# Gated mix of attention and an MLP: halves of value batches shared out over the turns of five, and the row-maximum product issued last in its slot

## The chip, the cores and the metric

The kernel runs on one core of one Trainium2 chip. The metric is the device time of one execution in microseconds (us), lower is better; the time given for the kernel is the median of its runs.

## The reference

```python
x = A_x                                             # 1 x 2048 x 448
g = sigmoid((x * gate_w).sum(-1, keepdims=True))
qkv = (x @ wqkv), split into q, k, v of 16 heads, 28 wide
p = softmax(q @ k.T * 28 ** -0.5)                   # per head, 2048 x 2048
a = (p @ v, heads side by side) @ wo
h = gelu(layernorm(x) @ w1 + b1)                    # 2048 x 1792, tanh form
b = h @ w2 + b2
out = g * a + (1 - g) * b
```

All inputs and outputs are 32-bit floats.

## The kernel before

The program has three stages. The first makes queries, keys and values; the second is the MLP; the third is the attention with the output projection. Each of the products of the first two stages is split into strips of 32 rows and mixed with row-maximum products by a planner (`Strips`). The change is in the third stage alone, from the function `early` on; what stands ahead of it in the program is the same.

**Units.** In the third stage the work of TensorE is written out by hand. The 16 heads form 4 groups of 4, the 2048 queries 4 chunks of 512. A *column* is one group with one chunk, and there are 16. A column holds 64 *units*: a unit is one head `j` of the group with one tile `k` of 128 keys, against the chunk's 512 queries, so 1024 units in all. Units are numbered `u`, with `j = u % 4`. Head `j` lies in the rows 32j to 32j+31 of the operands, so products of different heads use different row strips of TensorE.

**Scores.** A unit's scores are three products into one bank of PSUM: high part of the keys by high part of the queries (in traces `yh,ka` or `yh,kb`), low part of the keys by high of the queries (`yh,la`, `yh,lb`), and high of the keys by low of the queries (`yl,ka`, `yl,kb`). The first of the three has one row more than the head's 28, in which minus one meets the row's maximum, so that what lands in the bank is the score less its maximum. ScalarE then writes the exponentials of two or three banks at once to a tile `p` (L1164).

**Row maxima.** The maximum of each row of scores over all keys must be known before the column's scores are used. It comes from a product of its own, without splitting (L212, `kd,qd`), into one bank, which VectorE reduces (L214). Such a product with its reduction is called a *row maximum* here. `lone` (L1118) issues one, if its operands are loaded.

**Turns.** `turn_of` (L1131) takes the next 5 units, or 6 where fewer row maxima are still owed, or 7 where none are. The first half of the turn holds three units (four of seven), the second the others. Each half makes three passes over its units, one for each of the three products, then one exponential of the half's banks. Half and pass give six *slots*, 0 to 5. `extra` (L1146) names the slots of a turn that hold a row maximum, the head (from `u`) and the bank: in a turn of five slots 0, 3 and 5, in bank 6, the sixth of the score banks, and bank 6 again; in a turn of six slots 0 and 5, both in bank 6; in a turn of seven none. Scores use banks 0 to 5, values bank 7.

**Values.** A *batch* (L1169) is the four units of one tile of keys: four products of 32 columns of values (the stationary operand) by the units' exponentials, each into its own 32 partitions of bank 7, summed over the 16 tiles of keys of the column. A batch can be issued in two halves of 256 queries each. In the trace every value product appears as two records, so a batch is 8 records with 512 elements, a half batch 8 records with 256. After the last batch of a column `valued` copies the bank out on VectorE (L1026), sends the row of sums through DRAM (L1027, L1035, L1037 on SyncE's queue), and multiplies by its reciprocal on GpSimd (L1043).

**The order around the change.** The loop at L1181 takes a turn, runs what is due in that turn (`agenda`: loads, splits of keys and queries, closings of columns), then issues batches. `before` is the number of units that stood scored before this turn; a batch is open when its four units are among them. `quota` counts half batches. In turns of six and seven it is 3, or 4 when more than two batches are open; in turns of five it stays at 99, so every open batch is issued. After the last batch of a column the turn issues no more. The exponentials' tiles come from a pool with three buffers for each half (L955), so the tile of a turn takes the place of that of three turns before.

Each engine runs its own instructions in order, and waits for another by a semaphore; a waiting instruction holds up those behind it on its engine.

Of the kernel before, what the change touches and what calls it, by code (L numbers as in the profile page):

```python
# [35 lines left out]
def kernel(ctx: ExitStack, tc: tile.TileContext, xt, wqk, wv, wo, xk, w1, b1, w2, b2,  # L36
# [367 lines left out]
    class Strips:  # L404
# [28 lines left out]
        def at(self, t, fn, **uses):  # L433
            self.tasks.append((t, self.count, fn, uses))
            self.count += 1
# [473 lines left out]
    for b, m in enumerate((0, 3, 4)):  # L909
        x = QK(0, m)  # L910
# [32 lines left out]
    def turn_bank(i):  # L943
        return (i + shift) % 6

    def idle(n, b):
        for _ in range(n):
            nc.tensor.matmul(bk[:, b], khi[0][:, 0:P], khi[0][:, 0:CH], start=True, stop=True)  # L948
# [50 lines left out]
    def products(po, tt, groups):  # L999
        c, i = divmod(tt, TPC)  # L1000
        sl = slice(i * P, (i + 1) * P)
        for g in groups:
            h, l = (t[:, g, sl] for t in ohs[c])
            nc.tensor.matmul(po, h, woh[:, g], start=(g == 0), stop=False, skip_group_check=True)  # L1004
            nc.tensor.matmul(po, h, wol[:, g], start=False, stop=False, skip_group_check=True)  # L1005
            nc.tensor.matmul(po, l, woh[:, g], start=False, stop=(g == NG - 1), skip_group_check=True)  # L1006
# [7 lines left out]
    def project(tt):  # L1014
        po = bk[:, 6, :D]
        products(po, tt, range(NG))
        put(po, tt)
# [60 lines left out]
    def begun(n, turn):  # L1078

        g, c = divmod(n, NC)  # L1080
        if n + 1 < NG * NC:
            for j in range(4):
                at(turn + 1 + j // 2, lambda j=j: fetch_qq(n + 1, j))
            at(turn + 5, lambda: split_qq(n + 1))
            at(turn + 7, lambda: load_ms(n + 1))
        if c == (0 if g == 0 else 2) and g < NG - 1:
            for j in range(4):
                at(turn + 2 + j, lambda j=j: fetch_kk(g + 1, j))
                at(turn + 8 + j, lambda j=j: split_kk(g + 1, j))
            at(turn + 13, lambda: key_row(g + 1))  # L1090
            for t in range(2):
                at(turn + 9 + t, lambda t=t: load_v(g + 1, slice(8 * t, 8 * t + 8)))
        if g == NG - 1:
            for i in range(TPC):
                at(turn + 7 + i, lambda i=i: fetch_acc(c, i))
                at(turn + 9 + i // 2, lambda i=i: weigh_acc(c, i))
            for x in range(NG - 1):
                at(turn + 4 + x, lambda x=x: split_o(x, c, ot[x][:, c * CH:(c + 1) * CH]))
# [19 lines left out]
    def lone(s, b, turn):  # L1118
        if not rowmax.ready(s) or turn < cold[s]:
            return  # L1120
        for kind, n, j in rowmax.one(s, bk[:, b]):
            if kind == "q":
                at(turn + 1, lambda n=n, j=j: rowmax.load_q(n, j))
            elif kind == "k":
                at(turn + 1, lambda n=n, j=j: rowmax.load_k(n, j))
                cold[j] = turn + 4
            else:
                at(turn + 1, lambda n=n: rowmax.close(n))
                at(turn + 2, lambda n=n: rowmax.store(n))

    def turn_of(u, turn):  # L1131

        left = UNITS - u
        owed = rowmax.left()
        size = 5 if owed and owed > 2 * ((left - 116) // 6) else 6
        if not owed and not (tail and tail[0][0] <= turn + 1):
            size = 7
        size = min(left, size)
        na = min(4 if size == 7 else 3, size)
        nb = size - na  # L1140
        for x in range(u, u + size):
            n = x // 64
            if n not in begins:
                begins.add(n)
                begun(n, turn)
        extra = {5: ((0, 3, 6), (3, 1, 5), (5, 2, 6)), 6: ((0, 3, 6), (5, 2, 6))}.get(size, ())  # L1146
        place = (lambda i: i) if size == 7 else turn_bank
        for half, first, count in ((0, 0, na), (1, na, nb)):
            for p in range(3):
                for x, o, b in extra:  # L1150
                    if x == 3 * half + p:
                        lone((u + o) % 4, b if b == 6 else turn_bank(b), turn)
                for i in range(first, first + count):
                    n, k = divmod(u + i, 64)
                    k, j = divmod(k, 4)
                    r = slice(32 * j, 32 * j + DH + (p == 0))
                    ks = slice(k * P, (k + 1) * P)
                    w = (khi, klo, khi)[p][n // NC]
                    q = (qh, qh, ql)[p][n % 3]
                    nc.tensor.matmul(bk[:, place(i)], w[r, ks], q[r], start=(p == 0), stop=(p == 2), skip_group_check=True)  # L1160
            if count:
                t = ap.tile([P, 4 - half, CH], F32, name=f"p{half}")
                b = place(first)
                nc.scalar.activation(t[:, :count], bk[:, b:b + count], AF.Exp, scale=SCALE)  # L1164
                for i in range(count):
                    prob[u + first + i] = t[:, i]
        return size

    def batch(b, turn, sl=slice(0, CH)):  # L1169
        n, k = divmod(b, NT)  # L1170
        for j in range(4):
            nc.tensor.matmul(bk[32 * j:32 * j + 32, 7, sl], vg[n // NC][:, k, 32 * j:32 * j + 32], prob[4 * b + j][:, sl],  # L1172
                             start=(k == 0), stop=(k == NT - 1), skip_group_check=True)
        if k == NT - 1 and sl.stop == CH:
            valued(n, turn)
            return True
        return False

    u = b = turn = 0
    begun_half = False  # L1180
    while b < UNITS // 4:  # L1181
        before, quota = u, 99
        if u < UNITS:
            u += turn_of(u, turn)
            if u - before > 5:
                quota = 3 + (before // 4 - b > 2)
        for fn in agenda.pop(turn, ()):
            fn()
        if turn == 0:
            idle(6, 7)  # L1190
        if before == UNITS:
            products(bk[:, 6, :D], (NC - 1) * TPC, range(NG - 1))
            before = u = UNITS
        while 4 * b + 4 <= before and quota:
            if quota == 1 and not begun_half:
                if b % NT:
                    batch(b, turn, slice(0, CH // 2))
                    begun_half = True
                break
            last = batch(b, turn, slice(CH // 2 if begun_half else 0, CH))  # L1200
            quota -= 1 if begun_half else 2
            b, begun_half = b + 1, False
            if last:
                break
        if tail and tail[0][0] <= turn:
            project(tail.pop(0)[1])
        turn += 1
# [53 lines left out]
```

## Time and profile before

| | us |
|---|---|
| median of 3 runs | 1086.65 |
| lowest and highest | 1086.04, 1089.5 |
| the profiled execution | 1087.38 |
| its span, first to last instruction | 1085.6 |
| third stage, first units to the end of the span | about 452 to 1085.6 |
| of that, turns of five | about 452 to 822, the last three of them among turns of six |
| turns of six | about 803 to 978 |
| granted clock of TensorE | 0.999 |

In the rows below, PE is TensorE's matmuls, PEld its weight loads, DVE VectorE, ACT ScalarE, POOL GpSimd, SP SyncE. A row in order of time has the start in the span and the duration in us, then the engine, the line, the operation, what it writes from what it reads, the shape, and how many of the same kind were merged; in brackets stands the time for which the engine was idle before, and what ended it. "PEld ... [0.15 <-DVE mx L214]" is a weight load before which loads had paused 0.15 us until a reduction of VectorE was through.

### The profile page before, as it was taken

The numbers are of one execution on the slowest core, as the hardware profiler recorded it, in microseconds if no ns is written. First come the engines' busy times: TensorE is split into PE (matmuls) and PEld (weight loads), VectorE is DVE, ScalarE is ACT, GpSimd is POOL, SyncE is SP. The second block draws the span as 40 slices with busy tenths as digits, with TensorE's granted clock in tenths as the row PEclk, the third lists the DMA queues.
The fourth block names the chain that finished last, engine by engine and source line by source line (L and its number), as shares of the span: only waits on it lengthen the run. The fifth ranks groups of instructions, "written<-read, shape, count | busy, mean of one in ns | idle before, by whom it ended". The sixth has DMA issues, their size and how long they took to land.

```text
span 1085.6 us, 31067 instructions
## 1 busy us (share of the span) xinstructions
PE 1068.0 (98%) x13450; PEld 724.0 (67%) x13450; DVE 740.1 (68%) x1186; ACT 633.3 (58%) x652; POOL 367.7 (34%) x388
## 2 busy tenths in 40 slices
PE   9999999999999999999999999999999999999997
PEld 7999999999999999844444444444444444454655
DVE  4899898999999999866766656676664444420102
ACT  5343463043142142387888787788788888857571
POOL 4665577336234037341001101310110314444431
PEclk9999999999999999999999999999999999999999
DMA  7696433212100104320101011310110202011112
GB/s 242 212 282 214 148 111 107 71 46 61 45 7 7 46 20 109 96 72 19 27 8 27 16 32 37 91 33 1 30 33 19 63 23 58 26 47 38 60 46 67
DMA packets 47785, 73.20 MB, mean 67 GB/s; under 512 B 13840, under 2 KB 28816, under 8 KB 46848
## 3 DMA queue, kind: packets, MB, share of 16 engines
q1 hardware_dynamic: 33888, 39.11, 12.6%
q0 software_dynamic: 5120, 16.89, 5.6%
q10 hardware_dynamic: 8640, 15.21, 3.9%
q8 instruction: 105, 1.72, 0.7%
q14 instruction: 32, 0.26, 0.1%
HBM read 51.75 MB, written 19.31 MB: 65 GB/s over the span
## 4 chain that ended last, share of the span: by engine, by line
PE 94%; ACT 2%; DMA 1%; issue 1%; DVE 1%; SPq 0%; DVEq 0%; ACTq 0%
PE bk L488 35%; PE bk L1172 21%; PE bk L1160 18%; PE bk L212 15%; ACT p L1164 2%; PE bk L1004 1%; PE bk L1006 1%; PE bk L1005 1%; PE bk L920 1%; DMA gbs<-gb 1%; DMA first<-in_xt 0%; DVE acc L1011 0%; DMA kd<-qk 0%; DVE ob L1026 0%; PE bk L948 0%
## 5 line engine op out<-in xcount | busy, mean ns | idle before, releaser
L214 DVE TENSOR_REDUCE mx<-bk 128x1 f32<-128x512 f32 x1024 | 673.8, 688 | 221.6 <-PE bk L212 181.5
L1164 ACT ACTIVATE p<-bk 128x1536 f32<-128x1536 f32 (+2 forms) x379 | 480.8, 1322 | 129.6 <-PE bk L1160 128.0
L212 PE MATMUL bk<-kd,qd 28*128 28x512 f32 x1024 | 448.9, 440 | 3.6 <-DVE acc L1011 1.6
L212 PEld LDWEIGHTS bk<-kd,qd 28*128 28x128 f32 x1024 | 185.7, 182 | 183.4 <-DVE mx L214 114.2
L488 PE MATMUL bk<-yh,w1f 32*128 32x512 f32 x1568 | 192.7, 393 | 1.4 <-ACT gb L398 1.4
L488 PE MATMUL bk<-yl,w1f 32*128 32x512 f32 x784 | 167.2, 391 | 0.0
L488 PEld LDWEIGHTS bk<-yh,w1f 32*128 32x128 f32 x1568 | 154.0, 183 | 4.1 <-ACT gb L398 2.5
L488 PE MATMUL bk<-w2h,hh 32*128 32x448 f32 x896 | 145.4, 366 | 0.9 <-issue 0.9
L488 PE MATMUL bk<-w2l,hh 32*128 32x448 f32 x896 | 144.4, 364 | 0.0
L1172 PE MATMUL bk<-p,va 128*32 128x512 f32 (+1 forms) x1120 | 130.2, 564 | 0.0
L1172 PE MATMUL bk<-p,vb 128*32 128x512 f32 (+1 forms) x1208 | 129.0, 535 | 0.0
L363 POOL TENSOR_TENSOR hl<-h,hh 128x512 fp32r<-128x512 f32 x56 | 72.4, 1306 | 137.6 <-ACT hh L356 99.8
L488 PEld LDWEIGHTS bk<-yl,w1f 32*128 32x128 f32 x784 | 105.3, 183 | 0.4
L488 PEld LDWEIGHTS bk<-w2h,hh 32*128 32x128 f32 x896 | 102.8, 183 | 1.7 <-issue 1.3
L488 PEld LDWEIGHTS bk<-w2l,hh 32*128 32x128 f32 x896 | 102.8, 183 | 0.3
L1160 PE MATMUL bk<-yh,ka 29*128 29x512 f32 x512 | 101.5, 483 | 0.6 <-ACT p L1164 0.6
L840 POOL CAST yh<-yl 128x512 fp32r<-128x512 f32 x16 | 9.8, 611 | 269.5 <-PE bk L1160 96.5
L1160 PE MATMUL bk<-yh,kb 29*128 29x512 f32 x512 | 97.0, 479 | 2.3 <-ACT p L1164 2.3
L488 PE MATMUL bk<-w2h,hl 32*128 32x448 f32 x896 | 93.4, 363 | 0.0
L398 ACT ACTIVATE gb<-bk 128x448 f32<-128x448 f32 x14 | 7.6, 544 | 137.7 <-PE bk L488 131.4
L1160 PE MATMUL bk<-yh,la 28*128 28x512 f32 x512 | 83.6, 392 | 0.0
L1160 PE MATMUL bk<-yl,ka 28*128 28x512 f32 x512 | 82.8, 409 | 0.0
(141 smaller groups left out, 1602.1 us busy)
## 6 DMA issues: line engine op xcount, KB each, us to landing
qk<-qo ACTq DMA_DIRECT2D x28, 256.0 KB
raw<-in_xt SPq DMA_DIRECT2D x17, 256.0 KB
vs<-vt ACTq DMA_DIRECT2D x16, 256.0 KB
rc<-rls SPq DMA_DIRECT2D x60, 64.0 KB
bxr<-in_xk POOLq DMA_DIRECT2D x8, 448.0 KB, 5.9
acc<-gbs SPq DMA_DIRECT2D x16, 224.0 KB
out_y<-acc SPq DMA_DIRECT2D x16, 224.0 KB
qd<-qk SPq DMA_DIRECT2D x60, 56.0 KB
```

The costliest lines, as they stand in the source:

```text
L212: nc.tensor.matmul(ps, self.qd[n % 2][r, i * P:(i + 1) * P], self.kd[r, k * 512:(k + 1) * 512], start=True, stop=True)
L214: nc.vector.reduce_max(self.mx[n % 2][:, j, i, k:k + 1], ps, axis=AX)
L363: nc.gpsimd.tensor_sub(hl[f], h, hh[f].bitcast(F32))
L488: mm = nc.tensor.matmul(bk[:, x.bank, :n], a, b, start=x.first, stop=(len(x.rem) == 1 and m == len(ops) - 1), skip_group_check=True)
L840: nc.gpsimd.tensor_copy(h, l.bitcast(F32))
L920: nc.tensor.matmul(bk[:, b], w, v, start=(i == 0), stop=(i == len(ops) - 1), skip_group_check=True)
L1004: nc.tensor.matmul(po, h, woh[:, g], start=(g == 0), stop=False, skip_group_check=True)
L1005: nc.tensor.matmul(po, h, wol[:, g], start=False, stop=False, skip_group_check=True)
L1006: nc.tensor.matmul(po, l, woh[:, g], start=False, stop=(g == NG - 1), skip_group_check=True)
L1160: nc.tensor.matmul(bk[:, place(i)], w[r, ks], q[r], start=(p == 0), stop=(p == 2), skip_group_check=True)
L1164: nc.scalar.activation(t[:, :count], bk[:, b:b + count], AF.Exp, scale=SCALE)
L1172: nc.tensor.matmul(bk[32 * j:32 * j + 32, 7, sl], vg[n // NC][:, k, 32 * j:32 * j + 32], prob[4 * b + j][:, sl], start=(k == 0), stop=(k = ...
```

## The change

The diff has two edits. The first moves the loop over `extra` in `turn_of` behind the loop over the units: a slot's row maximum is issued after the slot's score products instead of ahead of them. Slots, heads and banks of the row maxima stay.

The second gives turns of five a quota: 3 half batches where the turn starts at a unit number that leaves 0 or 1 modulo 4, otherwise 2, and one more if more than that many plus two are open.

```diff
@@ turn_of
             for p in range(3):
-                for x, o, b in extra:
-                    if x == 3 * half + p:
-                        lone((u + o) % 4, b if b == 6 else turn_bank(b), turn)
                 for i in range(first, first + count):
...
                     nc.tensor.matmul(bk[:, place(i)], w[r, ks], q[r], start=(p == 0), stop=(p == 2), skip_group_check=True)
+                for x, o, b in extra:
+                    if x == 3 * half + p:
+                        lone((u + o) % 4, b if b == 6 else turn_bank(b), turn)
@@ the loop over turns
             if u - before > 5:
                 quota = 3 + (before // 4 - b > 2)
+            elif u - before == 5:
+                quota = 2 + (before % 4 < 2)
+                quota += 2 * (before // 4 - b) - begun_half > quota + 2
```

Both programs have the same number of turns, of the same sizes, with the same row maxima. The lines of the changed kernel are shifted: its score products are L1157.

A plain turn of five on TensorE, early in the stage, before the change (DVE_49 is VectorE's semaphore, Activation_49 ScalarE's):

```order
L212 MATMUL bk<-kd,qd_153 128x512 [waits DVE_49]
L1160 MATMUL bk<-yh,ka 128x512 [waits Activation_49]
L1160 MATMUL bk<-yh,ka 128x512 x2
L1160 MATMUL bk<-yh,la 128x512 x3
L1160 MATMUL bk<-yl,ka 128x512 x3
L212 MATMUL bk<-kd,qd_153 128x512
L1160 MATMUL bk<-yh,ka 128x512 [waits Activation_49]
L1160 MATMUL bk<-yh,ka 128x512
L1160 MATMUL bk<-yh,la 128x512 x2
L212 MATMUL bk<-kd,qd_153 128x512 [waits DVE_49]
L1160 MATMUL bk<-yl,ka 128x512 x2
```

The same turn on TensorE after it, with the first of its value products:

```order
L1157 MATMUL bk<-yh,ka 128x512 [waits Activation_49]
L1157 MATMUL bk<-yh,ka 128x512 x2
L212 MATMUL bk<-kd,qd_153 128x512 [waits DVE_49]
L1157 MATMUL bk<-yh,la 128x512 x3
L1157 MATMUL bk<-yl,ka 128x512 x3
L1157 MATMUL bk<-yh,ka 128x512 [waits Activation_49]
L1157 MATMUL bk<-yh,ka 128x512
L212 MATMUL bk<-kd,qd_153 128x512
L1157 MATMUL bk<-yh,la 128x512 x2
L1157 MATMUL bk<-yl,ka 128x512 x2
L212 MATMUL bk<-kd,qd_153 128x512 [waits DVE_49]
L1172 MATMUL bk<-p_9980,va 32x512 x2
```

The first row maximum has moved behind three score products, the middle one behind two, of which the first waits for ScalarE, and the last one behind the two last score products, to stand right ahead of the values.

The end of a turn of five in the fifth column on TensorE, before (four value products make a batch; `p_` numbers are exponentials' tiles):

```order
L212 MATMUL bk<-kd,qd_153 128x512 [waits DVE_49]
L1160 MATMUL bk<-yl,kb 128x512 x2
L1172 MATMUL bk<-p_11512,vb 32x512 x2
L1172 MATMUL bk<-p_11535,vb 32x512 x2
L212 MATMUL bk<-kd,qd_153 128x512 [waits DVE_49]
```

And the end of the same turn after:

```order
L1157 MATMUL bk<-yl,kb 128x512 x2
L212 MATMUL bk<-kd,qd_153 128x512 [waits DVE_49]
L1172 MATMUL bk<-p_11525,vb 32x256
L1172 MATMUL bk<-p_11548,vb 32x256 x3
L1172 MATMUL bk<-p_11560,vb 32x256 x2
L1172 MATMUL bk<-p_11583,vb 32x256 x2
L1157 MATMUL bk<-yh,kb 128x512 [waits Activation_49]
```

One whole batch has become the second half of one batch and the first half of the next.

The end of the turn of five that starts at 682.82 us in the trace of before, on TensorE, before the change:

```order
L212 MATMUL bk<-kd,qd_152 128x512 [waits DVE_49]
L1160 MATMUL bk<-yl,kb 128x512 x2
L1172 MATMUL bk<-p_12230,vb 32x512
L1172 MATMUL bk<-p_12251,vb 32x512 x3
L212 MATMUL bk<-kd,qd_152 128x512 [waits DVE_49]
```

And after it:

```order
L1157 MATMUL bk<-yl,kb 128x512 x2
L212 MATMUL bk<-kd,qd_152 128x512 [waits DVE_49]
L1172 MATMUL bk<-p_12322,vb 32x256 x3
L1172 MATMUL bk<-p_12334,vb 32x256
L1157 MATMUL bk<-yh,kb 128x512 [waits Activation_49]
```

A column closes here with a half batch, so the turn issues one half batch instead of a whole batch.

## The prediction

> **What bounds the kernel now.** I read the profile page first, for the engines and the costliest groups, then busy time by stage, then the waits, then single turns in order of time.
>
> ```profile
> PE 1068.0 (98%) x13450; PEld 724.0 (67%) x13450; DVE 740.1 (68%) x1186; ACT 633.3 (58%) x652; POOL 367.7 (34%) x388
> L214 DVE TENSOR_REDUCE mx<-bk 128x1 f32<-128x512 f32 x1024 | 673.8, 688 | 221.6 <-PE bk L212 181.5
> 452.00:822.00 370.00, 368.18 (x3493) 170.14 (x3495) 246.64 (x391) 296.28 (x250) 53.73 (x55) 1.00 0.14 37
> PEld bk L212 <- DVE mx L214: 110.2, 232, 0.8
> ```
>
> TensorE is busy for 98% of the span, and for 368.18 of the 370 us (third row) in which the turns of five stand. But such busy time holds a matmul that is queued as well as one that streams, so it doesn't say what sets the length of a turn. The waits do: weight loads of the row-maximum products (L212) wait 110.2 us for VectorE's reduction, 232 times. So I take one plain turn apart, the one from 567.07.
>
> ```profile
> 564.38 0.49 PE L212 MATMUL bk<-kd,qd 28*128 28x512 f32 x1
> 565.49 2.37 ACT L1164 ACTIVATE p<-bk 128x1536 f32<-128x1536 f32 x2 [0.37 <-PE bk L1160]
> 567.07 0.50 PE L212 MATMUL bk<-kd,qd 28*128 28x512 f32 x1
> 567.08 0.50 PE L1160 MATMUL bk<-yh,ka 29*128 29x512 f32 x3
> 567.61 1.99 DVE L214 TENSOR_REDUCE mx<-bk 128x1 f32<-128x512 f32 x3 [0.70 <-PE bk L212]
> 567.90 0.18 PEld L1160 LDWEIGHTS bk<-yh,ka 29*128 29x128 f32 x2
> 568.16 2.37 ACT L1164 ACTIVATE p<-bk 128x1536 f32<-128x1536 f32 x2 [0.30 <-PE bk L1160]
> 568.36 0.18 PEld L212 LDWEIGHTS bk<-kd,qd 28*128 28x128 f32 x1 [0.15 <-DVE mx L214]
> 568.48 0.39 PE L1160 MATMUL bk<-yl,ka 28*128 28x512 f32 x2
> 568.80 1.06 PE L1172 MATMUL bk<-p,va 128*32 128x512 f32 x8
> 569.79 0.49 PE L212 MATMUL bk<-kd,qd 28*128 28x512 f32 x1
> 571.78 1.92 PE L1172 MATMUL bk<-p,va 128*32 128x512 f32 x16
> 573.63 0.50 PE L212 MATMUL bk<-kd,qd 28*128 28x512 f32 x1
> ```
>
> (Start and duration in us, engine, line; in brackets the idle time before and what ended it.) The first row maximum starts with the turn. Its reduction starts 0.54 later (567.61), takes 0.69 (688 ns in the page's row) of the 1.99 for three, and at 568.36 lets go the load of the last row maximum, which uses the same bank 6: 1.29 after the turn's start. From there 0.44 to the value products (568.80), and 0.99 more for one batch of them until the next turn (569.79). **1.29 + 0.44 + 0.99 = 2.72**: this ring, row maximum, reduction, row maximum, values, sets the turn (the one before it, from 564.38, takes 2.69; I use 2.70 as the mean). Two batches take 1.85 (571.78 to 573.63), so a half batch more costs 0.43.
>
> A second ring lies close beneath. ScalarE's two exponentials start 1.09 after the turn (568.16) and last 2.37, so they end at 3.46. The second half's scores of the next turn write the banks they read: the pair from 565.49 ends at 567.86, and those loads start at 567.90. From there it is 0.90 to the values (568.80). Over two turns this asks for 3.46 + 0.04 + 0.90 = 4.40, plus the values of the turn between: 5.39 for one batch, against 2 x 2.72 = 5.44.
>
> **The change part by part.**
>
> *Row maximum last in its slot.* The first one moves behind three score products, which are issued within the 0.01 between 567.07 and 567.08. Its reduction, and so the release of the last row maximum, moves by that much at most: 0 to 0.02 a turn, and I take 0.006. It isn't below nothing, since it can't start ahead of the turn. At the end of the turn the last scores no longer stand behind the wait at 568.36, but the last row maximum itself still does, and the values stand behind it. So the values start 1.29 + 0.44 after the turn as before: **the wait is kept; only what is queued behind it changes**, from two score products and the values to the values alone. Some 118 turns of five and 45 of six have it: 163 x 0.006 = **+1.0 us** (0 to 3.3).
>
> The middle row maximum moves behind score products that may wait for ScalarE (567.90). It then reduces some 0.13 later, and the third reduction, now due to end at 567.61 + 1.99 = 569.60, would end at about 569.73. The next turn's first row maximum needs it at 569.79. I count nothing; if the margin fails, 0.05 in each of 26 turns, 1.3 us.
>
> A little comes back where the last scores carry waits of their own, which stood behind the row maximum:
>
> ```profile
> 527.53 0.18 PEld L212 LDWEIGHTS bk<-kd,qd 28*128 28x128 f32 x1 [0.27 <-DVE mx L214]
> 527.61 0.21 PEld L1160 LDWEIGHTS bk<-yl,ka 28*128 28x128 f32 x2
> 528.07 1.06 PE L1172 MATMUL bk<-p,va 128*32 128x512 f32 x8
> ```
>
> The two loads come 0.08 after the row maximum's there instead of with it, and the values 0.54 after instead of 0.44. Such turns are few; for some four I take **-0.4 us** (0 to -0.8).
>
> *Half batches.* Instead of 2, 1, 1, 1 batches, four turns take 3, 3, 2, 2 half batches. The number of turns, and of row maxima in each, stays. What a half batch costs is seen in the turns of six, which take them already:
>
> ```profile
> 843.15 2.81 ACT L1164 ACTIVATE p<-bk 128x1536 f32<-128x1536 f32 x2 [0.34 <-PE bk L1160]
> 843.79 1.93 PE L1172 MATMUL bk<-p,va 128*32 128x256 f32 x24
> 847.37 1.50 PE L1172 MATMUL bk<-p,va 128*32 128x256 f32 x16
> 848.79 0.49 PE L212 MATMUL bk<-kd,qd 28*128 28x512 f32 x1
> ```
>
> A batch and a half takes 848.79 - 847.37 = 1.42. Two such turns take 2.84, and the two that they replace 1.85 + 0.99 = 2.84. So the sum stays; for 55 more batches cut in two I take 0.005 each, **+0.3 us** (0 to 1).
>
> The Trainium skill, "TensorE: Matmul & The Clock Gate", Part 3 ("The mechanism"), speaks against cutting: weight loads overlap matmuls in flight only where their row groups differ, and value products use all rows. By that rule each cut batch would lay two more groups of loads bare, and the sum would be that of the third rival. The rows differ from it: eight value loads start at 837.08 (below), within the first matmuls, and a half batch costs just half a batch.
>
> *ScalarE's stalls.* Where a turn of six with one batch is followed by another turn, ScalarE is late:
>
> ```profile
> 806.27 0.50 PE L212 MATMUL bk<-kd,qd 28*128 28x512 f32 x1
> 807.49 0.18 PEld L212 LDWEIGHTS bk<-kd,qd 28*128 28x128 f32 x1 [0.68 <-ACT p L1164]
> 808.39 1.92 PE L1172 MATMUL bk<-p,va 128*32 128x512 f32 x16
> ```
>
> Values start 2.12 after this turn instead of 1.73. There are three such turns between 803 and 822; with three half batches in the turns before them (0.43 more time) two of them lose the wait and one moves on: **-0.8 us** (-1.2 to 0).
>
> *What the new quota leaves over.* From the order of the changed program I counted half batches turn by turn. After a batch that closes a column, the turn stops there, so its remaining half is carried. From the fourth such closing on one or two half batches are always owed, until the last turns of five. Two things follow. First, three turns (where 682.82, 720.92 and 758.98 stand now) take a single half batch. The turns of six show one:
>
> ```profile
> 834.00 0.64 PE L1172 MATMUL bk<-p,va 128*32 128x256 f32 x8
> 834.81 0.18 PEld L212 LDWEIGHTS bk<-kd,qd 28*128 28x128 f32 x1 [0.65 <-DVE mx L214]
> 836.18 0.51 PE L1160 MATMUL bk<-yh,ka 29*128 29x512 f32 x3 [0.37 <-ACT p L1164]
> 837.08 1.92 PE L1172 MATMUL bk<-p,va 128*32 128x512 f32 x16
> 837.54 0.13 PEld L1172 LDWEIGHTS bk<-p,va 128*32 128x32 f32 x4 [0.30 <-issue]
> 838.23 1.45 ACT L1164 ACTIVATE p<-bk 128x1536 f32<-128x1536 f32 x1 [0.76 <-PE bk L1172]
> ```
>
> The half batch starts at 834.00 and would be through 0.99 - 0.43 = 0.56 later, but the next turn starts at 834.81, held by reduction and exponential: 0.25 lost, and I take 0.28 in a turn of five, whose values start a little sooner. Then ScalarE is late for the next turn's second half (0.10; in the row 0.37, behind the longer exponentials of six). Second, an exponential writes one of three buffers, and waits until the values that read it are through: here the one at 838.23 starts 1.15 after its turn's values (837.08), 0.76 late. In the changed order this falls on a whole batch in the turn after the first and in two places after the third of these; each makes the next turn late by 0.35, and once both exponentials wait, 0.83. Against it, the copy of a finished column holds up VectorE less there:
>
> ```profile
> 570.00 0.69 DVE L1026 COPY ob<-bk 128x512 f32<-128x512 f32 x1 [0.40 <-PE bk L1172]
> 571.34 0.18 PEld L212 LDWEIGHTS bk<-kd,qd 28*128 28x128 f32 x1 [0.47 <-DVE mx L214]
> ```
>
> The copy puts the last row maximum at 1.55 instead of 1.29 after its turn (569.79), 0.27 lost; behind a short turn it fits. The places: 0.28 + 0.10 + 0.35 - 0.27 = 0.46; 0.28 + 0.10 - 0.27 = 0.11; 0.28 + 0.10 + 0.83 + 0.11 + 0.35 - 0.27 = 1.40. Together **+1.9 us** (0 to 4). In the other turns with something owed only the first half batch must be through, and the turn from 842.07 shows that this is just in time: its exponentials run 2.81 without a gap though the second needs the first half batch of that turn.
>
> *Keys.* Where new keys load, TensorE waits:
>
> ```profile
> 656.69 0.47 PE L212 MATMUL bk<-kd,qd 28*128 28x512 f32 x1 [0.76 <-DMA kd<-qk]
> ```
>
> On SyncE's queue the four loads of a column's reciprocals now stand behind key loads that they stood ahead of. I take half of the 0.76, **-0.4 us** (-0.8 to +0.8).
>
> **Sum:** 1.0 - 0.4 + 0.3 - 0.8 + 1.9 - 0.4 = **+1.6 us**. The profiled execution took 1087.38 us, 1.8 more than its span, and would become 1089.0; the median of the runs shown, 1086.65, becomes 1088.2. That is within 0.3% (3.3 us), about what a measurement of this kernel can tell from no change. The terms' ends add up to -2 to +7 us if all fall on one side.
>
> **The rivals.**
>
> *The wait was the scores', and goes.* A turn without any row maximum shows what is then left:
>
> ```profile
> 647.03 0.50 PE L1160 MATMUL bk<-yh,kb 29*128 29x512 f32 x3
> 648.61 1.07 PE L1172 MATMUL bk<-p,vb 128*32 128x512 f32 x8
> ```
>
> Values start after 1.58 instead of 1.73. For it: 110.2 us of waits at the moved instruction. Against it: its own release at 1.29 and the 0.44 behind it, which the change leaves alone. ScalarE's ring would then bind: four turns take 4 x 1.58 + 4.82 = 11.14, of which the pair of one-batch turns must grow from 5.14 to 5.39, so 11.39 against 3 x 2.70 + 3.56 = 11.66 now. 30 such fours give -8 us, and in turns of six next to nothing: **1079 us**.
>
> *The exponentials' buffers decide: slower.* From the fourth closing on, 26 turns take two half batches of different batches, and half of them or more have an exponential that must wait for values of its own turn. I say just in time; the point is 2.43 + 0.04 after the turn's start. If it is a batch (1.73 + 1.15 = 2.88) and not half of one that must be through, the next turn is 0.4 late: 13 turns 5 us, 26 turns 10 us, **1093 to 1098 us**. For it: the 0.76 at 838.23. Against it: the unbroken pair at 843.15.
>
> *Loads of the cut batches lie bare.* 55 batches x 2 groups of 0.13 (837.54) = 14 us, **1102 us**. Against it stands 1.42. By the skill's rule named above, this would be the case.
>
> **How the numbers follow.** Forecast 0.68, the faster rival 0.13, the buffers 0.16, bare loads 0.03. Of the forecast 0.60 falls within 3.3 us, 0.06 above and 0.02 below. So faster 0.15, same 0.60, slower 0.25. The range 1083.0 to 1094.5 takes in the terms' ends (-2 to +7) with some room below, and most of the buffers' case; it leaves out the faster rival, the bare loads and the worst of the buffers, some 0.2 in all.
>
> **What would show it.** Right, if plain turns of five still put 1.70 to 1.74 between start and values, with the last row maximum's load at 1.28 to 1.31 after VectorE; if two half batches take 0.99 and three 1.42; and if three turns with a single half batch are followed by late ones. Wrong, if values start after 1.6 (first rival), if exponentials show idle time ended by value products in many turns between 610 and 800 (second), or if the first row maximum's reduction starts later than 0.56 after the turn.

## The result and the profile after

The changed kernel takes **1093.2 us** (median of 6 runs, 1091.6 to 1096.7) against 1086.35 for the kernel before beside it (6 runs, 1085.7 to 1089.5): a ratio of 1.0063, 95% interval 1.0048 to 1.0077. It is 6.9 us slower, where I had forecast 1.6 us and called no change the likeliest. The profiled execution took 1093.11 us with a span of 1091.3.

The page's row of the kernel before for the row-maximum loads comes first, as the one below is to be compared with it. Then, for the changed kernel, the page's first row, three of its groups, and the busy time of the stretch of the turns of five:

```profile
L212 PEld LDWEIGHTS bk<-kd,qd 28*128 28x128 f32 x1024 | 185.7, 182 | 183.4 <-DVE mx L214 114.2
```

```profile
PE 1075.1 (99%) x13890; PEld 758.1 (69%) x13890; DVE 739.8 (68%) x1186; ACT 635.1 (58%) x652; POOL 367.4 (34%) x388
L214 DVE TENSOR_REDUCE mx<-bk 128x1 f32<-128x512 f32 x1024 | 673.4, 689 | 229.2 <-PE bk L212 183.2
L212 PEld LDWEIGHTS bk<-kd,qd 28*128 28x128 f32 x1024 | 185.6, 182 | 26.2 <-DVE mx L214 3.4
L1157 PEld LDWEIGHTS bk<-yh,ka 29*128 29x128 f32 x512 | 43.3, 181 | 80.8 <-ACT p L1164 65.6
452.00:822.00 370.00, 367.98 (x3884) 194.23 (x3880) 243.97 (x387) 293.80 (x247) 53.77 (x55) 1.00 0.13 37
```

The L212 row is the trap of this case. The wait of the row-maximum loads for VectorE, 114.2 us before (110.2 of it from 470 us on), reads 3.4 now, and the time rose. The last row maximum still waits as long. But a few score loads that stood behind it now run in that time, and each turn opens with a score load, so the idle time is booked to ScalarE (the waits of score loads for it go from 22.6 to 115.1 us) or to nobody. VectorE's own idle time ahead of the reductions rose from 221.6 to 229.2 us: it starts on them a little later.

A plain turn of the changed kernel, in order of time, to be laid beside the one from 567.07:

```profile
567.66 0.50 PE L1157 MATMUL bk<-yh,ka 29*128 29x512 f32 x3
567.67 0.18 PEld L212 LDWEIGHTS bk<-kd,qd 28*128 28x128 f32 x1
567.67 0.50 PE L212 MATMUL bk<-kd,qd 28*128 28x512 f32 x1
...
568.25 2.00 DVE L214 TENSOR_REDUCE mx<-bk 128x1 f32<-128x512 f32 x3 [0.78 <-PE bk L212]
...
568.99 0.18 PEld L212 LDWEIGHTS bk<-kd,qd 28*128 28x128 f32 x1
...
569.42 1.06 PE L1172 MATMUL bk<-p,va 128*32 128x512 f32 x8
570.41 0.19 PEld L1157 LDWEIGHTS bk<-yh,ka 29*128 29x128 f32 x3 [0.84 <-ACT p L1164]
```

The ring is the same and each of its pieces but one keeps its length: the reduction lets the last row maximum go at 568.99, the values follow 0.43 later and take 0.99. Only the first piece has grown: **the reduction starts 0.59 after the turn instead of 0.54**, though the row maximum's load is issued just 0.01 after it. So the last row maximum comes at 1.33 instead of 1.29 and the values at 1.76 instead of 1.73 in the turn shown before. Over about 100 plain turns of five in each trace, the reduction's mean start went from 0.531 to 0.585 and that of the values from 1.712 to 1.758.

Ahead of the turns of five, executions of the same work differ by up to 3 us (the second turn of five starts between 456.75 and 459.99). So single profiles are compared from that turn to the start of the last turn of six. Before and after (first and last row of each):

```profile
458.53 0.49 PE L212 MATMUL bk<-kd,qd 28*128 28x512 f32 x1
...
1055.95 0.53 PE L1160 MATMUL bk<-yh,kb 29*128 29x512 f32 x4
```

```profile
457.57 0.50 PE L1157 MATMUL bk<-yh,ka 29*128 29x512 f32 x3
...
1061.66 0.53 PE L1157 MATMUL bk<-yh,kb 29*128 29x512 f32 x4
```

That is 597.42 and 604.09: **+6.67 us lie in the turns**, nearly all that the medians differ by. This length is called "the turns" below.

### The profile page after: what moved, and what is told of

Its sections match the earlier page's. It is cut to its first block, busy times and chain, and to the rows that moved or that the text cites. A ratio compares the mean times of both kernels' runs of the same rounds, so it can differ in the third digit from the quotient of the medians.

```text
span 1091.3 us, 31954 instructions
## 1 busy us (share of the span) xinstructions
PE 1075.1 (99%) x13890; PEld 758.1 (69%) x13890; DVE 739.8 (68%) x1186; ACT 635.1 (58%) x652; POOL 367.4 (34%) x388
## 4 chain that ended last, share of the span: by engine, by line
PE 95%; ACT 3%; issue 1%; DMA 1%; DVE 0%; DVEq 0%; SPq 0%; ACTq 0%
PE bk L488 35%; PE bk L1157 27%; PE bk L1172 22%; PE bk L212 7%; ACT p L1164 2%; PE bk L1004 1%; PE bk L1006 1%; PE bk L1005 1%; PE bk L920 1%; DMA first<-in_xt 0%; DMA gbs<-gb 0%; DVE acc L1011 0%; PE bk L948 0%; ACT gb L398 0%; PE bk L905 0%
## 5 line engine op out<-in xcount | busy, mean ns | idle before, releaser
L214 DVE TENSOR_REDUCE mx<-bk 128x1 f32<-128x512 f32 x1024 | 673.4, 689 | 229.2 <-PE bk L212 183.2
L212 PE MATMUL bk<-kd,qd 28*128 28x512 f32 x1024 | 452.3, 444 | 0.8 <-DVE acc L1011 0.8
L212 PEld LDWEIGHTS bk<-kd,qd 28*128 28x128 f32 x1024 | 185.6, 182 | 26.2 <-DVE mx L214 3.4
L1172 PE MATMUL bk<-p,vb 128*32 128x256 f32 (+1 forms) x1472 | 129.4, 469 | 0.0
L1157 PE MATMUL bk<-yh,ka 29*128 29x512 f32 x512 | 105.9, 476 | 1.9 <-ACT p L1164 1.9
L1157 PE MATMUL bk<-yh,kb 29*128 29x512 f32 x512 | 99.6, 479 | 3.2 <-ACT p L1164 3.1
L1157 PEld LDWEIGHTS bk<-yh,ka 29*128 29x128 f32 x512 | 43.3, 181 | 80.8 <-ACT p L1164 65.6
L1157 PE MATMUL bk<-yh,la 28*128 28x512 f32 x512 | 89.6, 392 | 0.0
L1157 PE MATMUL bk<-yl,ka 28*128 28x512 f32 x512 | 89.2, 390 | 0.0
L1157 PEld LDWEIGHTS bk<-yh,kb 29*128 29x128 f32 x512 | 41.2, 181 | 68.9 <-ACT p L1164 49.6
```

The lines of the kernel that those rows point to most:

```text
L212: nc.tensor.matmul(ps, self.qd[n % 2][r, i * P:(i + 1) * P], self.kd[r, k * 512:(k + 1) * 512], start=True, stop=True)
L214: nc.vector.reduce_max(self.mx[n % 2][:, j, i, k:k + 1], ps, axis=AX)
```

## The experiments

My theory: the first row maximum's result comes some 0.046 later because its product is issued behind three score products, and the ring carries that through most of the 163 turns; the new quota is nearly neutral. The rivals: the quota's leftovers and cut batches; the places of the other two row maxima; and TensorE itself.

| kernel | median us | ratio to before (95%) | turns, us |
|---|---|---|---|
| before | 1086.35 | 1 | 597.42 |
| after | 1093.2 | 1.0063 (1.0048 to 1.0077) | 604.09 |
| new quota alone | 1087.7 | 1.0005 (0.9992 to 1.0017) | 598.47 |
| new order alone | 1092.1 | 1.0045 (1.0031 to 1.0060) | 603.24 |
| after, first row maximum back ahead | 1086.9 | 0.9997 (0.9988 to 1.0007) | 597.47 |
| after, first one behind one product | 1092.2 | 1.0042 (1.0028 to 1.0056) | 601.55 |
| after, first one behind two | 1092.7 | 1.0047 (1.0029 to 1.0065) | 602.65 |
| old quota, slots 3 and 5 moved | 1086.0 | 0.9987 (0.9979 to 0.9996) | 596.40 |
| before, half reductions | 1076.8 | 0.9918 (0.9903 to 0.9933) | 592.89 |
| after, half reductions | 1071.8 | 0.9863 (0.9850 to 0.9876) | 590.11 |
| new quota, half reductions | 1072.7 | 0.9866 (0.9843 to 0.9890) | 590.97 |
| first back ahead, quicker quota | 1084.6 | 0.9980 (0.9969 to 0.9992) | 595.15 |

Each ratio is to runs of the kernel before beside it, whose medians lay between 1086.2 and 1087.4. The turns come from one profiled execution of each kernel.

**The two halves of the change.** First the quota without the order: the loop over `extra` stands ahead of the score products again.

> The new quota with the row maxima in their old places. My theory: the slowdown is the first row maximum of a turn, whose reduction starts 0.58 instead of 0.53 us after the turn once its product is issued behind three score products; some 163 turns x 0.046 = 7.5 us, and the quota is worth -0.6 in all. So 1085.7 us (1084.5 to 1087.5), values 1.71 after the start of plain turns, and the three turns with a single half batch still there. Rival: the quota's leftovers and cut batches cost the 6.9 us; then 1093, with late turns in it that the trace of the change has too.

1087.7 us, not told apart from before; the turns +1.05. So the rival falls. My own figure, 1085.7, was too low by 2: I had put the quota at -0.6, and in the trace it costs 1.05.

Then the order without the quota:

```diff
-            elif u - before == 5:
-                quota = 2 + (before % 4 < 2)
-                quota += 2 * (before // 4 - b) - begun_half > quota + 2
```

> The row maxima last in their slots, with the old quota of 2, 1, 1, 1 batches. My theory: 1093.9 us (1092.5 to 1095), reduction 0.58 and values 1.757 after the start of plain turns of both sizes, turns of one batch 2.75, and the three late turns of 2.12 between 803 and 822 stay. Rival, the quota: as before, 1086 to 1087.

1092.1 us, a little below what I expected, and +5.82 in the turns. Plain turns have the reduction at 0.586 and the values at 1.7575; the late turns between 803 and 825 stay (values after 2.07 there). 1.05 and 5.82 add up to 6.87, against 6.67 for both together: the order is the cost.

**Which of the three row maxima.** In the changed kernel only slot 0's goes back:

```diff
+                for x, o, b in extra:
+                    if x == 3 * half + p == 0:
+                        lone((u + o) % 4, b if b == 6 else turn_bank(b), turn)
                 for i in range(first, first + count):
...
                 for x, o, b in extra:
-                    if x == 3 * half + p:
+                    if x == 3 * half + p > 0:
```

> The changed kernel, but the row maximum of slot 0 stands ahead of its score products again; those of slots 3 and 5 stay behind theirs. My theory: all of the cost hangs on slot 0, so 1085.7 us (1084 to 1087.5), reduction 0.53 to 0.54 and values 1.71 after a plain turn's start. Rival, the last row maximum or the middle one costs as well (what stands behind the wait changed, or the third reduction is late for the next turn): half of it stays, 1089 to 1090; all of it, 1093.

1086.9 us, and the turns are 597.47: **all of it, 6.62 us, hangs on slot 0**. A turn of this kernel:

```profile
567.04 0.50 PE L212 MATMUL bk<-kd,qd 28*128 28x512 f32 x1
567.58 0.69 DVE L214 TENSOR_REDUCE mx<-bk 128x1 f32<-128x512 f32 x1 [0.69 <-PE bk L212]
...
568.32 0.18 PEld L212 LDWEIGHTS bk<-kd,qd 28*128 28x128 f32 x1
...
568.77 1.07 PE L1175 MATMUL bk<-p,va 128*32 128x512 f32 x8
569.77 0.18 PEld L212 LDWEIGHTS bk<-kd,qd 28*128 28x128 f32 x1 [0.84 <-DVE mx L214]
```

The reduction is at 0.54 again, the last load at 1.28, the values at 1.73 (1.708 in the mean).

The other two places alone, with the old quota (the diff above, and that of the new order alone):

> The old quota, with the row maxima of slots 3 and 5 behind their products and that of slot 0 ahead. Against the kernel before it shows these two places alone. My theory: the last one frees the score products behind its wait, which I put at 0.4 us in all, and the middle one costs nothing, so 1086 to 1087 us, with values 1.708 after a plain turn. Rival, the middle row maximum pushes the third reduction into the next turn's first (0.05 in 26 turns): 1088 to 1088.5.

The turns are 1.0 us shorter than before, and 1086.0 is 0.13% below it: the two places together are worth a little, more than my 0.4. I put it down to the score products that no longer stand behind the last row maximum; no run separates the two. The rival with the third reduction falls: it does end later (it starts at 1.93 instead of 1.85), and the next turn's first reduction still starts at 0.535.

**How the delay grows with the products ahead.** Slot 0's row maximum behind the first of the three, and then behind the second (`i == 1`):

```diff
+                    if half == p == 0 and i == 0:
+                        for x, o, b in extra:
+                            if x == 0:
+                                lone((u + o) % 4, b, turn)
```

> The changed kernel, but the row maximum of slot 0 stands behind one of its three score products instead of behind all three. If the delay grows with each product issued ahead (0.046 / 3 = 0.015 a turn), the reduction starts 0.55 after the turn, values 1.725, and the time is 1088.2 us. If it is a step that any product ahead brings (the first product after the value products costs more), reduction 0.58, 1093. If only the fourth place is late, reduction 0.54, 1086.

> The changed kernel with the row maximum of slot 0 behind two of its three score products. Behind none its reduction starts 0.537 after its weight load, behind one 0.565, behind three 0.575. If most of the delay comes with the first product ahead: 0.565 to 0.575, values 1.74 to 1.757, 1091.5 to 1093 us. If the two steps are only scatter and each product adds the same: 0.562, 1090.5.

The row maximum's load and the reductions in one turn of each, behind one and behind two (0.57 and 0.58 apart):

```profile
563.58 0.18 PEld L212 LDWEIGHTS bk<-kd,qd 28*128 28x128 f32 x1
...
564.15 1.97 DVE L214 TENSOR_REDUCE mx<-bk 128x1 f32<-128x512 f32 x3 [1.13 <-PE bk L212]
```

```profile
563.76 0.18 PEld L212 LDWEIGHTS bk<-kd,qd 28*128 28x128 f32 x1
...
564.34 1.97 DVE L214 TENSOR_REDUCE mx<-bk 128x1 f32<-128x512 f32 x3 [1.21 <-PE bk L212]
```

Means over the plain turns of five:

| products ahead | reduction after the turn | values after the turn | turns, us |
|---|---|---|---|
| 0 (first row maximum back ahead) | 0.534 | 1.708 | 597.47 |
| 1 | 0.569 | 1.740 | 601.55 |
| 2 | 0.577 | 1.748 | 602.65 |
| 3 (after) | 0.585 | 1.758 | 604.09 |

It is a step of 0.035 with the first product ahead and 0.008 for each further one, and the turns follow: +4.1, +1.1, +1.4 us. (The medians behind one, two and three, 1092.2, 1092.7 and 1093.2, lie too close together to tell the last two steps apart.) So neither of my pure cases: not one slope, and not only a step. It is no matter of the fourth place.

**What the step is.** The trace records which products send a signal, that is, raise the count that VectorE and ScalarE wait on. Before, the three score products behind the first row maximum send none. After, the last product ahead of it does, because the row maximum carries a wait of its own and the count of what stands ahead of it is sent first. The one plain turn whose row maximum carries no wait bears this out: at 650.25 in the changed kernel no product ahead sends, and the reduction starts 0.543 after the row maximum's product (0.538 in the same turn behind one and behind two). The first row maxima of the turns separate by it (median time from the row maximum's product to the reduction, where VectorE was idle; 0.533 with nothing just ahead, 149 cases before):

| products just ahead | one sends | two send |
|---|---|---|
| 1 | 0.565 (149 cases) | |
| 2 | 0.569 (145) | 0.596 (4) |
| 3 | 0.573 (146) | 0.600 (3) |

To try the case in which none sends, the wait of the row maximum is taken over by an added product of 64 columns, so that the three score products stay where they are and send nothing:

```diff
     for j in range(4):
+        if j == 3 and end and u < UNITS and rowmax.ready((u + 3) % 4) and turn + 1 >= cold[(u + 3) % 4]:
+            rowmax.touch((u + 3) % 4, bk[:, 6])
```

> The changed kernel, with one more product of 64 columns into bank 6, whose result nothing reads, ahead of the last value product of each turn. It takes over the first row maximum's wait for VectorE, and then the third score product ahead of that row maximum no longer sends a signal of its own: the row maximum's signal counts for both. Order and number of the products at the turn's start stay. In the traces so far the reduction starts 0.573 us after its product where one signal is sent just ahead (three products, 152 cases), 0.600 where two are (3 cases), 0.565 behind one product with its signal (149 cases), 0.53 to 0.54 behind one or two products without any. If the signals are sent one after the other, each 0.027, and a product ahead costs 0.004: 0.533 + 3 x 0.004 = 0.545. If the products ahead cost it by streaming beside: 0.573 as before. The time is not at issue: the added product costs a switch between values and row maximum in each of some 160 turns (0.1 to 0.2 each, estimate from the 0.13 between groups of value loads), so 1105 to 1130 us.

```profile
641.14 0.51 PE L1165 MATMUL bk<-yh,ka 29*128 29x512 f32 x3
641.15 0.18 PEld L220 LDWEIGHTS bk<-kd,qd 28*128 28x128 f32 x1
641.15 0.49 PE L220 MATMUL bk<-kd,qd 28*128 28x512 f32 x1
...
641.70 1.98 DVE L222 TENSOR_REDUCE mx<-bk 128x1 f32<-128x512 f32 x3 [1.93 <-PE bk L220]
...
645.06 0.50 PE L1165 MATMUL bk<-yh,ka 29*128 29x512 f32 x3
```

The same three products ahead at the same distance, and the reduction 0.548 after the row maximum's product (148 cases, median) instead of 0.573. **The signal ahead is worth 0.025, the three products 0.015 together.** The time, 1246.5 us in one run against a forecast of 1105 to 1130, I had far too low: the added product waits for the third reduction and holds up the last value product (such a turn takes 645.06 - 641.14 = 3.92). It says nothing about the change.

On this the Trainium skill, "TensorE: Matmul & The Clock Gate", Part 3 ("The cost: per-tile semaphore tail"), has a rule: signals of products that run side by side are sent one after the other, 26.3 ns for each, and 4.7 ns for each product. The traces agree closely: an estimate by it gives 31, 36 and 40 ns more behind one, two and three products with one signal ahead, and measured are 32, 36 and 40 (0.565, 0.569 and 0.573 less 0.533). With the 0.01 between the issues this estimate comes to 0.05 a turn, what the first term of the prediction lacked.

**Does the delay act through the ring alone?** Reductions over 256 of the 512 columns, with the other half of the scores left out of the maxima, slacken the ring:

```diff
-            nc.vector.reduce_max(self.mx[n % 2][:, j, i, k:k + 1], ps, axis=AX)
+            nc.vector.reduce_max(self.mx[n % 2][:, j, i, k:k + 1], ps[:, :256], axis=AX)
```

> The kernel before, with each row-maximum reduction over 256 of its 512 columns, so half of the scores are left out of the maxima; all products stand as they did. It makes VectorE's part of the ring some 0.3 us shorter (estimate from 0.69 us for 512). If the ring row maximum, reduction, row maximum, values sets the turn of five, values start some 1.58 to 1.65 after the turn instead of 1.71 and the last row maximum waits for nothing; ScalarE then binds in the pairs of one-batch turns, and the turns of five (458.53 to 803.56, 345.0 us in the trace of before) take some 8 us less, 337; those of six are worth 0.1 in each of 39 where ScalarE lets them, 0 to 4. In all 1075 to 1080 us; what VectorE gives back ahead of 452 us isn't counted. If TensorE's own queue sets the turn, values stay at 1.71.

> The changed kernel with the same half reductions. My theory: the fourth place of the first row maximum costs time only through the ring, so with the ring slack its 0.046 a turn is gone: values 1.58 to 1.65 after the turn as in the kernel before with half reductions, and at most 2 us between the two. Rival: the order costs TensorE itself (more starts of products in a row, or the place of the last row maximum); then the 5 to 7 us between the two orders stay.

Four turns of the kernel before with half reductions (row maxima that open a turn, values, one wait for ScalarE):

```profile
571.55 0.50 PE L212 MATMUL bk<-kd,qd 28*128 28x512 f32 x1
...
573.35 1.93 PE L1172 MATMUL bk<-p,va 128*32 128x512 f32 x16
575.21 0.50 PE L212 MATMUL bk<-kd,qd 28*128 28x512 f32 x1
...
576.80 1.07 PE L1172 MATMUL bk<-p,va 128*32 128x512 f32 x8
577.80 0.50 PE L212 MATMUL bk<-kd,qd 28*128 28x512 f32 x1
...
578.72 0.18 PEld L1160 LDWEIGHTS bk<-yh,ka 29*128 29x128 f32 x2 [0.16 <-ACT p L1164]
...
579.62 1.07 PE L1172 MATMUL bk<-p,va 128*32 128x512 f32 x8
580.62 0.50 PE L212 MATMUL bk<-kd,qd 28*128 28x512 f32 x1
...
582.21 1.07 PE L1172 MATMUL bk<-p,va 128*32 128x512 f32 x8
583.20 0.49 PE L212 MATMUL bk<-kd,qd 28*128 28x512 f32 x1
```

Values start 1.80, 1.59, 1.82 and 1.59 after their turns, together 11.65 a four. The reduction takes 0.42 now, so VectorE no longer sets the turn; in every second one ScalarE does. That 1076.8 us lies in my range is luck: of the 10 us that the whole kernel gains, 8.9 lie ahead of the turns, which start at 449.60 instead of 458.53, and those I had not counted, while the turns of five, for which I expected some 8, gain 3.4 in all. And the changed kernel with half reductions:

```profile
569.80 0.51 PE L1157 MATMUL bk<-yh,ka 29*128 29x512 f32 x3
...
570.39 0.42 DVE L214 TENSOR_REDUCE mx<-bk 128x1 f32<-128x256 f32 x1 [1.01 <-PE bk L212]
...
571.38 1.50 PE L1172 MATMUL bk<-p,va 128*32 128x512 f32 x16
572.81 0.51 PE L1157 MATMUL bk<-yh,ka 29*128 29x512 f32 x3
...
574.40 1.50 PE L1172 MATMUL bk<-p,va 128*32 128x256 f32 x16
575.83 0.51 PE L1157 MATMUL bk<-yh,ka 29*128 29x512 f32 x3
...
577.41 1.07 PE L1172 MATMUL bk<-p,va 128*32 128x512 f32 x8
578.41 0.51 PE L1157 MATMUL bk<-yh,ka 29*128 29x512 f32 x3
...
580.23 1.07 PE L1172 MATMUL bk<-p,va 128*32 128x512 f32 x8
```

The first reduction is still late (0.59), and the values come after 1.58, 1.59, 1.58 and 1.82 all the same: with slack in the ring the late reduction costs nothing. That bears the theory out. But the changed kernel is now faster, by 2.8 us in the turns and 5.0 in the medians, where I had given at most 2. Which half of the change does that?

> The new quota with the row maxima in their old places and reductions over 256 of 512 columns (half of the scores left out of the maxima). It tells which part made the changed kernel with half reductions some 5 us faster than the kernel before with them. If the quota: a turn of a batch and a half between two turns gives ScalarE's ring (4.40 plus the values between) the time that a one-batch turn lacks, so values start 1.60 after the turn in three of four turns and 1.80 in one, against two and two with the old quota: 0.2 in each of 26 fours, 1071 to 1073 us. If the order (score products no longer queued behind the last row maximum): 1077, and 1.80 in every second turn.

The quota: 1072.7 us and 590.97 in the turns, with one turn in four at 1.80. Laid beside this run, the changed kernel with half reductions differs in the order alone, and takes 590.11: with slack in the ring the order costs nothing. **Evened-out values do help ScalarE's ring**, by 592.89 - 590.97 = 1.9 us, as soon as that ring is the one that binds. In the full kernel it isn't.

**A version below both.** The first row maximum ahead, the other two behind, and the leftovers taken up sooner:

```diff
-                quota += 2 * (before // 4 - b) - begun_half > quota + 2
+                quota += 2 * (before // 4 - b) - begun_half > quota + 1
```

> The row maximum of slot 0 ahead of its products, those of slots 3 and 5 behind, and a quota that takes the third half batch when more than quota + 1 are owed instead of quota + 2. So what a closing column leaves is taken up within some four turns, nothing stays owed for long, and one single-half turn is left instead of three. From the late turns of the kernel with the first row maximum back (651.18, 687.09, 764.70, 771.00, 822.86: 2.6 us over 1.71) and the short turns' 0.25 each I expect some 2 us less than it: 1085 us (1084 to 1086.5), about 0.2% below the kernel before. If the leftovers cost nothing: 1086.9 as there.

1084.6 us, 0.2% below the kernel before, interval clear of 1. The late turns that the leftovers made (651, 687, 765 and 771 in the kernel that it is compared with) are gone, and the turns are 2.3 us shorter than before.

## Why the prediction was off, point by point

1093.2 us lies inside the range that I gave, 1083.0 to 1094.5, but that is luck. Its upper end was there for many terms at their worst at once, and for the case of the exponentials' buffers; neither happened. The terms of the quota came out near their sum, and the first term alone, given as 0 to 3.3, makes up nearly all of the time. Of my signs of being right, two failed (plain turns of five have 1.76 between start and values, not 1.70 to 1.74, and the last row maximum's load at 1.33, not 1.28 to 1.31), and one of being wrong came true.

**The failed step** is the first term of the change: that the first row maximum's reduction "moves by that much at most: 0 to 0.02 a turn, and I take 0.006". It moved by 0.054 in the mean, and the values behind it by 0.046. I took the distance between issues, 0.01, for the delay of the result, and this is only a fifth of it: the rest is the signal sent just ahead (0.025) and the products that end beside it (0.015). The path of the term was right, from the reduction through the ring to the values, and its count of turns nearly so; its size was not: +1.0 forecast, +6.6 measured (604.09 - 597.47), with values 0.050 later (1.708 to 1.758) in the plain turns, some 140 of the 163. The others wait for something else: where a copy lies in the turn, the values come after 1.98 before and 1.97 after. I had named the sign for it, a reduction later than 0.56 after the turn, and gave no price for it.

**"The wait is kept; only what is queued behind it changes"** was right, and with it the case against the first rival. But that rival's price was too good as well: with the ring slack, the turns of five and six shrink by 4.5 us in the old order and quota (597.42 to 592.89), not by 8. I had let ScalarE stretch one pair of turns in four; it stretches two (values after 1.80 and 1.82), so a four takes 11.65, about what I had for the full kernel (11.66).

**The middle and the last row maximum**, 0 and -0.4: measured -1.0 together (596.40 - 597.42).

**The quota's terms** were 0.3 - 0.8 + 1.9 - 0.4 = +1.0; measured +1.05. The pieces are in the trace as well. A single half batch and what comes of it:

```profile
683.94 0.51 PE L1157 MATMUL bk<-yh,kb 29*128 29x512 f32 x3
...
685.70 0.64 PE L1172 MATMUL bk<-p,vb 128*32 128x256 f32 x8
686.52 0.50 PE L1157 MATMUL bk<-yh,kb 29*128 29x512 f32 x3 [0.17 <-ACT p L1164]
...
688.34 1.06 PE L1172 MATMUL bk<-p,vb 128*32 128x512 f32 x8
689.33 0.50 PE L1157 MATMUL bk<-yh,kb 29*128 29x512 f32 x3
689.48 2.39 ACT L1164 ACTIVATE p<-bk 128x1024 f32<-128x1024 f32 x2 [0.43 <-PE bk L1172]
...
691.45 0.64 PE L1172 MATMUL bk<-p,vb 128*32 128x512 f32 x4
```

The short turn takes 2.58, where 2.75 - 0.43 = 2.32 would do: 0.26 lost, forecast 0.28. The exponential at 689.48 then waits for a whole batch, and the values of that turn come 2.12 after it instead of 1.76: 0.36, forecast 0.35. Behind the third short turn, from 761.77, the turn from 764.35 holds up the next one by 0.80, forecast 0.83. The other turns with something owed are just in time, so the rival of the exponentials' buffers, whose 1093 to 1098 holds the measured time, was not the cause: it gave the right size by another road. Between 803 and 830 one late turn is left of three, as forecast (from 827.04, values after 2.10). The key wait of 0.76 is gone altogether (I took half): the row maximum at 656.98 follows its turn's scores without a gap. But in the turn ahead of it an exponential now waits, and its values come after 2.12 instead of 1.58; the two turns up to that point (from 650.25, and from 649.60 before) take 6.72 instead of 7.09. So 0.37 is left of the 0.76, and my half was right by luck. Loads of cut batches don't lie bare: two half batches take 1.00 and three 1.43.

With the terms as measured, -1.0 + 1.05 + 6.62 = 6.67 us: the sum is closed. (The quota costs as much in the other order: 597.47 - 596.40 = 1.07.) The chances leaned on the small first term, which I took from the distance between issues; I looked for no row that bounds how late a result comes when other products stand just ahead. With 0.046 in that term slower would have been the likeliest.

## What to carry to other kernels

Where a ring through another engine sets the pace, the instruction that feeds that engine goes first, ahead even of work issued within 0.01 us of it: 0.05 us in each of some 140 turns was nearly the whole result. When a wait's row in the profile shrinks by 97% and the span grows, look at when the engine that was waited for starts: the label had moved to other loads, the wait had not. And an even spread of work over turns pays only once the ring that it relieves is the one that binds; it was worth 1.9 us there and cost 1 here.

## What the runs showed of the hardware

VectorE starts on a product's result later when a product just ahead sends a signal too: 0.565 to 0.573 us after the product's issue with one such signal, 0.596 to 0.600 with two (few cases), 0.533 with nothing ahead and 0.548 behind three products that send none. Where signals are sent is decided, in these programs, by waits: a row maximum that carries a wait has the product ahead of it send the count so far, in all plain turns here, and the one without a wait (650.25) has not. So a wait can cost time though it has long been met.
